# A gated feed-forward kernel: low parts of w_out computed by GpSimd, their smaller copy by ScalarE, and the matmul of w_out's bound placed two units later

## The chip, the cores and the metric

The kernel runs on one core of one Trainium2 chip. The metric is the device time of one execution in microseconds: the median of three runs of the kernel before is 1093.89 us (1093.72 to 1094.65). Where the text speaks of engines, TensorE does matmuls, VectorE and ScalarE do elementwise work, GpSimd is the slower elementwise engine (POOL in the profile), and SyncE issues the DMAs (SP). Each engine works through its own list of instructions in order; an instruction whose operand is not ready holds up all that stand behind it.

## What is computed

Two steps follow each other. The first mixes seven neighbouring rows of `x` with softmax weights, for each of 8 groups of 24 columns; the second is a feed-forward layer with a sigmoid gate.

```
w   = softmax(weight_gen, axis=-1)                 # [4, 4096, 8, 7]
out[b, s, h, :] = sum_k w[b, s, h, k] * x_pad[b, s + k, h, :]
y   = out.reshape(16384, 192)
h   = y @ w_in                                     # [16384, 2048]
g   = h / (1 + exp(-1.702 * h))
res = g @ w_out                                    # [16384, 192]
```

`w_in` (192 x 2048) and `w_out` (2048 x 192) arrive as 64-bit floats, the rest as 32-bit floats.

## The kernel before

The 16384 rows are cut into 32 blocks of 512. A block's mixed rows (tile `acc`) are made by GpSimd as seven products and six additions of 128 x 768 elements (`attend`, L150 and L165); its softmax (`softmax`, L129 to L144) wanders over VectorE (maximum, sum, reciprocal), GpSimd (subtract, multiply) and ScalarE (exponential). `scales` finds the block's largest magnitude on VectorE (L235 to L208), spreads it over all partitions by one small TensorE matmul into a tile `top` (L211), and makes scale factors of it. `split_x` and `turn` then write the block as pairs of half-precision numbers and transpose it by DMA.

The hidden layer is computed in units: unit (block, f) is one slice of 128 of the 2048 hidden columns, 16 units to a block. The text counts the units of block 0 from 0: unit 8 is slice 8. For each unit TensorE does four matmuls in `whole` (L390 to L393) and one in `halves` (L401 or L402) into a PSUM tile `h`; `gate` makes the tanh on ScalarE (`th`, L407) and the gated value on VectorE (`h`, L408); `split` writes it as two half-precision parts, the high one by ScalarE (`g`, L413) and the low one by VectorE (`g`, L414); and `second` multiplies these with three half-precision versions of `w_out`: `wos`, `wol` and `woh` (L424 to L426, 12 matmuls a unit). `woh` is `w_out` scaled and rounded, `wol` what the rounding left, and `wos` is `woh` times 2^-12.

The units go in groups of four: `whole` of the first and second, `halves` of all four, `gate` of the first, and so on. From the third group on, the matmuls of `second` for earlier units are put between them. The tiles `h` and `top` share a pool of five PSUM buffers.

All other work is put between the steps of the units by a table of numbers: `plan((2.3, 3.05, 3.1), bound_out())` means that the first step of `bound_out` is written into the program behind the point 2.3 units after the start, its second at 3.05, and so on. `until(n + 0.7)` in the loop over groups takes from the table what is due. So the table alone sets the order of the instructions on every engine.

`w_out` is prepared in six pieces of 512 columns. `narrow` makes 32-bit floats of the 64-bit ones, in the upper words of `raw_o`, so that a float lies in every second word; it also sums magnitudes. `bound_out` makes of these sums one scale factor `to_out` for all of `w_out`: VectorE reductions, the small matmul L211 into `top`, and a few VectorE operations on single columns (L216 to L352). Then `parts_out(c)` makes the three versions of piece c: `woh` by ScalarE (L357), `wol` by VectorE (L359), `wos` by VectorE (L377). All this stands between units 2 and 8 of block 0, where `second` first needs it.

Pairs of blocks share a tile `wb` of softmax weights; that of blocks 2 and 3 is subtracted by GpSimd (L131, once for each block) and exponentiated by ScalarE (L133, twice) while units 4 to 8 run, and `attend(2)` starts on GpSimd when the softmax of block 2 is done.

Of the kernel before, what the change touches and what calls it, by code (L numbers as in the profile page):

```python
# [14 lines left out]
AF = mybir.ActivationFunctionType  # L15
ALU = mybir.AluOpType
# [6 lines left out]
def conv_attention_then_ffn(  # L23
# [8 lines left out]
    nc = tc.nc  # L32
# [38 lines left out]
    woh, wol, wos = (const.tile([P, NF * D], F16, name=n) for n in ("woh", "wol", "wos"))  # L71
# [120 lines left out]
    scale = {}  # L192
    inv_w, unit = sc[:, 0:1], sc[:, 1:2]
    to_in, to_out = sc[:, 2:3], sc[:, 3:4]
# [24 lines left out]
    def power(e, to, inv, top):  # L219

        nc.vector.tensor_scalar(to.bitcast(I32), e, -1.0, top * ONE, ALU.mult, ALU.add)
        nc.vector.tensor_scalar(to.bitcast(I32), to.bitcast(I32), ONE, 253 * ONE, ALU.max, ALU.min)
        nc.vector.tensor_scalar(inv.bitcast(I32), to.bitcast(I32), -1.0, 254 * ONE, ALU.mult, ALU.add)
# [92 lines left out]
    narrowed = {}  # L316
# [21 lines left out]
    def bound(a0, a1, e):  # L338
        nc.vector.tensor_reduce(tops[1][:, 0:1], sums[:, a0:a1], axis=AX.X, op=ALU.max)
        yield from top_of(tops[1], e, True)  # L340
# [6 lines left out]
    def bound_out():  # L347

        e = sums[:, 14:15].bitcast(I32)
        yield from bound(6, 12, e)  # L350
        power(e, to_out, unit, 267)
        nc.vector.tensor_scalar(unit, unit, inv_w, 2.0**11, ALU.mult, ALU.mult)  # L352

    def parts_of(key, to, hi, lo):

        f = narrowed[key]
        nc.scalar.activation(hi, f, AF.Copy, scale=to)  # L357
        yield
        nc.vector.scalar_tensor_tensor(lo, f, to, hi, ALU.mult, ALU.subtract)  # L359

    def parts_in(c):
        s = slice(c * QC, (c + 1) * QC)
        yield from parts_of(("i", c), to_in, w0h[:, s], w0l[:, s])
# [8 lines left out]
                nc.sync.dma_start(to[h], tail[0][h * C1 : (h + 1) * C1, s].rearrange("d (q k) -> d q k", k=P))  # L372

    def parts_out(c):
        s = slice(c * QC, (c + 1) * QC)
        yield from parts_of(("o", c), to_out, woh[:, s], wol[:, s])
        nc.vector.tensor_scalar(wos[:, s], woh[:, s], 2.0**-12, None, ALU.mult)  # L377


    hp, th, gg, po, osb = {}, {}, {}, {}, {}  # L380
# [63 lines left out]
    def plan(slots, gen):  # L444
        for n in slots:
            todo.setdefault(math.floor(n), []).append((n, len(todo), gen))
# [20 lines left out]
    with tc.manual_schedule():  # L467
# [47 lines left out]
        plan((-2.5, -1.4), parts_tail(1))  # L515
        plan((-1.9, -0.7), parts_in(2))
        plan((-1.2, -0.06), parts_in(3))
        plan((2.3, 3.05, 3.1), bound_out())
        for c, slots in enumerate(((3.2, 3.6), (3.7, 4.1), (4.2, 4.7), (5.2, 5.7), (6.2, 6.7), (7.2, 7.7))):
            plan(slots, parts_out(c))  # L520
        plan((8.0,), scales_out(0))
        plan((8.2, 9.6, 9.7), scales(1))
# [121 lines left out]
```

## Time and profile before

| what | value |
|---|---|
| median of three runs | 1093.89 us |
| the profiled execution, its own time | 1095.54 us |
| its span | 1093.6 us |
| TensorE busy | 1053.7 us, 96% |
| VectorE, ScalarE, GpSimd busy | 834.6, 721.3 and 711.2 us |
| chain that ended last | 92% TensorE, 3% VectorE, 2% GpSimd, 2% ScalarE |

The profiled execution lies 1.94 us above its span and 1.65 us above the median. In the page's table of 40 slices TensorE is busy nine tenths or more from the third slice on, so the stretch before about 100 us is where other engines set the pace.

### The profile page before, as it was taken

What the parts mean: (1) busy time and instruction counts of PE and PEld (TensorE: products, weight loads), DVE (VectorE), ACT (ScalarE), POOL (GpSimd) and SP (SyncE); (2) the same over time, 40 slices, a digit from 0 to 9 for tenths busy, and PEclk for the clock granted to TensorE, in tenths of its full rate; (3) what the DMA queues carried; (4) which work ended last, traced back from release to release, by engine and by line L of the source; (5) the groups of instructions that cost most, each with busy time, mean ns of one, the idle gap of its engine ahead of it and who ended that gap; (6) DMA issues with size and microseconds to landing.
All of it is one profiled execution on the core that took longest, in us unless ns stands there. A gap on an engine that the chain in (4) does not pass through costs nothing.

```text
span 1093.6 us, 22203 instructions
## 1 busy us (share of the span) xinstructions
PE 1053.7 (96%) x8821; PEld 726.0 (66%) x8821; DVE 834.6 (76%) x1562; ACT 721.3 (66%) x1245; POOL 711.2 (65%) x483
## 2 busy tenths in 40 slices
PE   5399999999999999999999999999999999999998
PEld 4156666667676766666666666666666676767666
DVE  8787777787777777777778777777777777788765
ACT  5765766666666666666666666666666666666665
POOL 4439786666876666886666687666678766698000
PEclk9699999999999999999999999999999999999999
DMA  9300310312031021302112121121312102110110
GB/s 313 113 7 27 91 32 18 91 32 92 16 91 33 18 91 33 88 18 76 34 33 91 33 80 27 44 65 32 92 30 77 33 20 89 33 30 18 32 32 16
DMA packets 73232, 60.72 MB, mean 56 GB/s; under 512 B 60588, under 2 KB 65964, under 8 KB 71592
## 3 DMA queue, kind: packets, MB, share of 16 engines
q1 hardware_dynamic: 73128, 59.30, 18.9%
q8 instruction: 69, 1.13, 0.4%
q14 instruction: 35, 0.29, 0.1%
HBM read 31.96 MB, written 12.58 MB: 41 GB/s over the span
## 4 chain that ended last, share of the span: by engine, by line
PE 92%; DVE 3%; POOL 2%; ACT 2%; issue 1%; DMA 0%; POOLq 0%; ACTq 0%
PE o L424 16%; PE o L426 15%; PE o L425 15%; PE h L391 10%; PE h L392 10%; PE h L390 10%; PE h L393 10%; PE h L401 6%; POOL acc L165 1%; POOL prod L150 1%; PE tr L183 1%; DVE h L408 1%; ACT abs L336 1%; DVE g L414 0%; ACT bits L326 0%
## 5 line engine op out<-in xcount | busy, mean ns | idle before, releaser
L424 PE MATMUL o<-wos,g 128*128 128x192 f16 x2048 | 504.9, 247 | 0.0
L426 PE MATMUL o<-woh,g 128*128 128x192 f16 x2048 | 503.7, 246 | 0.0
L425 PE MATMUL o<-wol,g 128*128 128x192 f16 x2048 | 503.7, 246 | 0.0
L414 DVE SCALAR_TENSOR_TENSOR g<-g,h 128x512 f16<-128x512 f16 x512 | 340.1, 684 | 155.3 <-ACT g L413 147.0
L413 ACT ACTIVATE g<-h 128x512 f16<-128x512 f32 x512 | 305.7, 597 | 190.8 <-DVE h L408 190.7
L407 ACT ACTIVATE th<-h,s 128x512 f32<-128x512 f32 x512 | 337.0, 683 | 128.8 <-PE h L402 128.8
L408 DVE SCALAR_TENSOR_TENSOR h<-th,h 128x512 f32<-128x512 f32 x512 | 341.8, 690 | 82.9 <-ACT th L407 82.9
L165 POOL TENSOR_TENSOR acc<-acc,prod 128x768 f32<-128x768 f32 x186 | 338.1, 1817 | 14.6
L150 POOL TENSOR_TENSOR prod<-xb,wb 128x768 f32<-128x768 f32 x186 | 287.8, 1547 | 9.6
L424 PEld LDWEIGHTS <-g 128*128 128x128 f16 x2048 | 200.0, 98 | 97.6 <-issue 53.0
L425 PEld LDWEIGHTS <-g 128*128 128x128 f16 x2048 | 200.3, 98 | 40.9
L426 PEld LDWEIGHTS <-g 128*128 128x128 f16 x2048 | 200.3, 98 | 0.0
L390 PE MATMUL h<-xt,w0l 128*128 128x512 f16 x512 | 195.0, 381 | 0.5 <-DMA xt<-xs 0.5
L391 PE MATMUL h<-xt,w0h 128*128 128x512 f16 x512 | 195.1, 381 | 0.0
L392 PE MATMUL h<-xt,w0h 128*128 128x512 f16 x512 | 195.0, 381 | 0.0
L393 PE MATMUL h<-xt,wth 128*128 128x512 f16 x512 | 194.8, 380 | 0.0
L131 POOL TENSOR_TENSOR wb<-wb,wm 128x224 f32<-128x224 f32 x31 | 18.3, 592 | 237.4 <-DVE wm L129 237.4
L392 PEld LDWEIGHTS <-w0h 128*128 128x128 f16 x512 | 50.3, 98 | 61.0 <-issue 1.1
L393 PEld LDWEIGHTS <-wth 128*128 128x128 f16 x512 | 50.3, 98 | 61.0 <-issue 1.1
L402 PE MATMUL h<-xd,tl 64*128 64x512 f16 x256 | 77.7, 383 | 1.0 <-DVE g L414 1.0
L401 PE MATMUL h<-xt,tl 64*128 64x512 f16 x256 | 77.4, 383 | 0.0
L390 PEld LDWEIGHTS <-w0l 128*128 128x128 f16 x512 | 50.3, 98 | 3.0 <-issue 1.7
(91 smaller groups left out, 514.7 us busy)
## 6 DMA issues: line engine op xcount, KB each, us to landing
xb<-in_x_dram SPq DMA_DIRECT2D x12, 1344.0 KB, 6.3
out_dram<-osb SPq DMA_DIRECT2D x31, 384.0 KB, 2.6
wb<-in_weight_gen_dram SPq DMA_DIRECT2D x16, 224.0 KB, 3.2
ro<-in_moe_w_out_dram SPq DMA_DIRECT2D x4, 768.0 KB, 12.1
xb<-in_x_dram SPq DMA_DIRECT2D x3, 768.0 KB, 7.9
ri<-in_moe_w_in_dram SPq DMA_DIRECT2D x4, 512.0 KB, 8.2
xb<-in_x_dram SPq DMA_DIRECT2D x4, 504.0 KB, 5.9
xd<-xt SPq DMA_DIRECT2D x31, 64.0 KB, 2.1
```

The lines of the kernel that those rows point to most:

```text
L165: nc.gpsimd.tensor_tensor(acc, acc, t, ALU.add)
L390: nc.tensor.matmul(ps, lhsT=w0l[:, s], rhs=x0, start=start, stop=False)
L391: nc.tensor.matmul(ps, lhsT=w0h[:, s], rhs=x2, start=False, stop=False)
L392: nc.tensor.matmul(ps, lhsT=w0h[:, s], rhs=x0, start=False, stop=False)
L393: nc.tensor.matmul(ps, lhsT=th_[:, s], rhs=x1, start=False, stop=stop)
L407: nc.scalar.activation(t, hp[u], AF.Tanh, scale=scale[u[0]][:, 4:5])
L408: nc.vector.scalar_tensor_tensor(hp[u], t, 1.0, hp[u], ALU.add, ALU.mult)
L413: nc.scalar.activation(g[:, 0], hp[u], AF.Copy, scale=2.0**-12)
L414: nc.vector.scalar_tensor_tensor(g[:, 1], g[:, 0], -(2.0**12), hp.pop(u), ALU.mult, ALU.add)
L424: nc.tensor.matmul(o, lhsT=lo, rhs=wos[:, d], start=a and j % 2 == 0, stop=False, skip_group_check=True)
L425: nc.tensor.matmul(o, lhsT=hi, rhs=wol[:, d], start=False, stop=False, skip_group_check=True)
L426: nc.tensor.matmul(o, lhsT=hi, rhs=woh[:, d], start=False, stop=z, skip_group_check=True)
```

## The change

`parts_out` no longer goes through `parts_of`. ScalarE now first scales the piece in place in `raw_o`, then rounds it to `woh`, and later makes `wos` of it; GpSimd subtracts `woh` from the scaled piece, which gives `wol`. VectorE has no part in it any more. In the table of places, the second and third step of `bound_out`, which hold the matmul L211 and the single-column operations, go from 3.05 and 3.1 to 4.2 and 4.21, and the places of the six pieces go with them.

```diff
     def parts_out(c):
+
         s = slice(c * QC, (c + 1) * QC)
-        yield from parts_of(("o", c), to_out, woh[:, s], wol[:, s])
-        nc.vector.tensor_scalar(wos[:, s], woh[:, s], 2.0**-12, None, ALU.mult)
+        f = narrowed["o", c]
+        nc.scalar.activation(f, f, AF.Copy, scale=to_out)
+        nc.scalar.activation(woh[:, s], f, AF.Copy)
+        nc.gpsimd.tensor_tensor(wol[:, s], f, woh[:, s], ALU.subtract)
+        yield
+        nc.scalar.activation(wos[:, s], woh[:, s], AF.Copy, scale=2.0**-12)
...
-        plan((2.3, 3.05, 3.1), bound_out())
...
+        plan((2.3, 4.2, 4.21), bound_out())
...
```

Below the edit, lines of the changed kernel carry numbers that are higher by 5 (the tanh is L412 instead of L407, the high part L418 instead of L413). On TensorE the matmul L211 of `bound_out` stood directly ahead of unit 4's `whole`; it now stands behind `whole` of units 4 and 5 and `halves` of units 4 to 7. On VectorE the softmax maximum of block 3 and the gated value of unit 4 now stand ahead of L216 to L352. The next lists show ScalarE and GpSimd; the names end in the number of the buffer.

ScalarE, before, from the high part of unit 3 (`h_428`) to the tanh of unit 6; `h_493`, `h_498` and `h_503` are units 4, 5 and 6:

```order
L413 ACTIVATE g_475<-h_428 128x512
L357 ACTIVATE woh_97<-ro_112,sc_100 128x512 x2
L407 ACTIVATE th_509<-h_493,s_284 128x512
L357 ACTIVATE woh_97<-ro_112,sc_100 128x512
L407 ACTIVATE th_515<-h_498,s_284 128x512
L413 ACTIVATE g_518<-h_493 128x512
```

ScalarE in the changed kernel, from the same place; units 4 and 5 are `h_481` and `h_486` here:

```order
L418 ACTIVATE g_475<-h_428 128x512
L412 ACTIVATE th_497<-h_481,s_284 128x512
L378 ACTIVATE ro_112<-ro_112,sc_100 128x512
L379 ACTIVATE woh_97<-ro_112 128x512
L382 ACTIVATE wos_99<-woh_97 128x512
L412 ACTIVATE th_512<-h_486,s_284 128x512
L418 ACTIVATE g_515<-h_481 128x512
```

The tanh of unit 4 has moved ahead of the pieces of `w_out`, and each piece has three instructions in place of one, the second and third of which read what the one before them writes.

ScalarE, before, at the end of the stretch, from the tanh of unit 7 (`h_504`) to the tanh of unit 8 (`h_565`) and the exponentials of blocks 3 and 2 (`wb_137`, in this order):

```order
L407 ACTIVATE th_547<-h_504,s_284 128x512
L357 ACTIVATE woh_97<-ro_112,sc_100 128x512
L413 ACTIVATE g_553<-h_504 128x512
L357 ACTIVATE woh_97<-ro_112,sc_100 128x512
L133 ACTIVATE wb_137<-wb_137 128x224
L407 ACTIVATE th_607<-h_565,s_284 128x512
L133 ACTIVATE wb_137<-wb_137 128x224
```

ScalarE in the changed kernel there, from the second step of the fifth piece on; unit 7 is `h_492`, unit 8 `h_571`:

```order
L379 ACTIVATE woh_97<-ro_112 128x512
L418 ACTIVATE g_557<-h_492 128x512
L382 ACTIVATE wos_99<-woh_97 128x512
L378 ACTIVATE ro_112<-ro_112,sc_100 128x512
L379 ACTIVATE woh_97<-ro_112 128x512
L382 ACTIVATE wos_99<-woh_97 128x512
L133 ACTIVATE wb_137<-wb_137 128x224
L412 ACTIVATE th_613<-h_571,s_284 128x512
L133 ACTIVATE wb_137<-wb_137 128x224
```

The exponentials and the tanh of unit 8 still stand behind all pieces, of which each is now three instructions long.

GpSimd, before, from the last two additions for block 1 (`acc_256`) to the first product for block 2 (`acc_629`); `wm_523` belongs to block 2, `wm_490` to block 3:

```order
L165 TENSOR_TENSOR acc_256<-acc_256,prod_411 128x768
L150 TENSOR_TENSOR prod_414<-xb_119,wb_117 128x768
L165 TENSOR_TENSOR acc_256<-acc_256,prod_414 128x768
L131 TENSOR_TENSOR wb_137<-wb_137,wm_523 128x224
L131 TENSOR_TENSOR wb_137<-wb_137,wm_490 128x224
L144 TENSOR_TENSOR wb_137<-wb_137,wr_524 128x224
L150 TENSOR_TENSOR acc_629<-xb_139,wb_137 128x768
```

GpSimd in the changed kernel; `wm_521` belongs to block 2, `wm_478` to block 3:

```order
L165 TENSOR_TENSOR acc_256<-acc_256,prod_414 128x768
L380 TENSOR_TENSOR wol_98<-ro_112,woh_97 128x512 x2
L131 TENSOR_TENSOR wb_137<-wb_137,wm_521 128x224
L380 TENSOR_TENSOR wol_98<-ro_112,woh_97 128x512 x4
L131 TENSOR_TENSOR wb_137<-wb_137,wm_478 128x224
L144 TENSOR_TENSOR wb_137<-wb_137,wr_522 128x224
L150 TENSOR_TENSOR acc_635<-xb_139,wb_137 128x768
```

The subtraction for block 3, for which the first of the two exponentials waits, has come to stand behind the low parts of all six pieces.

## Rows read from the trace of the kernel before

**Rows 1.** Busy time of each engine in two stretches: length, busy time and instructions of PE, PEld, DVE, ACT and POOL, then the granted TensorE clock as a share of full speed, the share of the DMA engines and GB/s.

```profile
54.00:58.10 4.10, 4.10 (x12) 1.04 (x11) 2.35 (x10) 1.56 (x3) 0.00 (x0) 0.52 0.00 0
...
99.00:1090.00 991.00, 990.85 (x8402) 685.09 (x8402) 755.27 (x1394) 657.76 (x1127) 659.74 (x435) 1.00 0.17 48
```

**Rows 2.** Waits of TensorE between 40 and 110 us: who waited for whom, us in total, times, longest.

```profile
PE top L211 <- DVE tf L206: 6.6, 1, 6.6
PE top L211 <- DVE tf L208: 3.6, 2, 1.9
```

**Rows 3.** TensorE in order of time: start in us, length, what it did, and in brackets how long the engine had been idle and who released it. The matmul at 46.71 is the last of units 0 to 3, the one at 68.22 the last of unit 10, that at 72.90 the last of unit 11.

```profile
46.71 0.38 PE L393 MATMUL h<-xt,wth 128*128 128x512 f16 x1
...
53.67 0.19 PE L211 MATMUL top<-tf,ones 128*128 128x4 bf16 x1 [6.58 <-DVE tf L206]
...
68.22 0.38 PE L393 MATMUL h<-xt,wth 128*128 128x512 f16 x1
...
70.24 0.18 PE L211 MATMUL top<-tf,ones 128*128 128x1 bf16 x1 [1.64 <-DVE tf L208]
...
72.90 0.38 PE L393 MATMUL h<-xt,wth 128*128 128x512 f16 x1
...
96.84 0.38 PE L393 MATMUL h<-xt,wth 128*128 128x512 f16 x1
...
99.16 0.18 PE L211 MATMUL top<-tf,ones 128*128 128x1 bf16 x1 [1.94 <-DVE tf L208]
```

**Rows 4.** The chain that ended last, in order of time: start, length, what. Between the first two of these rows the chain has GpSimd rows only.

```profile
73.04 0.58 POOL wb L144
...
95.84 1.81 POOL acc L165
97.68 0.96 DVE top L235
```

**Rows 5.** VectorE in order of time. The row at 53.52 is the low part of unit 3, that at 68.05 the gated value of unit 8; L222 finishes the factor `to_out`.

```profile
53.52 0.68 DVE L414 SCALAR_TENSOR_TENSOR g<-g,h 128x512 f16<-128x512 f16 x1
54.12 0.15 DVE L216 TENSOR_REDUCE tm<-top 128x1 f32<-128x4 f32 x1
...
54.68 0.15 DVE L222 TENSOR_SCALAR sc<-sc 128x1 int32<-128x1 int32 x1
...
56.52 0.38 DVE L129 TENSOR_REDUCE wm<-wb 128x32 f32<-128x224 f32 x1
...
68.05 0.69 DVE L408 SCALAR_TENSOR_TENSOR h<-th,h 128x512 f32<-128x512 f32 x1
...
77.79 0.37 DVE L129 TENSOR_REDUCE wm<-wb 128x32 f32<-128x224 f32 x1
```

**Rows 6.** ScalarE in order of time. The tanh at 67.27 is that of unit 8, the one at 74.56 that of unit 11.

```profile
52.86 0.60 ACT L413 ACTIVATE g<-h 128x512 f16<-128x512 f32 x1 [0.78 <-DVE h L408]
54.87 1.39 ACT L357 ACTIVATE woh<-ro,sc 128x512 f16<-128x512 f32 x2 [1.42 <-DVE sc L222]
...
58.51 0.75 ACT L357 ACTIVATE woh<-ro,sc 128x512 f16<-128x512 f32 x1
59.16 0.67 ACT L407 ACTIVATE th<-h,s 128x512 f32<-128x512 f32 x1
59.73 0.59 ACT L413 ACTIVATE g<-h 128x512 f16<-128x512 f32 x1
60.21 0.76 ACT L357 ACTIVATE woh<-ro,sc 128x512 f16<-128x512 f32 x1
...
66.99 0.39 ACT L133 ACTIVATE wb<-wb 128x224 f32<-128x224 f32 x1
67.27 0.68 ACT L407 ACTIVATE th<-h,s 128x512 f32<-128x512 f32 x1
...
74.56 0.68 ACT L407 ACTIVATE th<-h,s 128x512 f32<-128x512 f32 x1
```

**Rows 7.** ScalarE's groups of instructions by line and shape: count, busy us, mean ns of one, idle time before.

```profile
L413 ACT ACTIVATE g<-h 128x512 f16<-128x512 f32 x512 | 305.7, 597 | 190.8 <-DVE h L408 190.7
...
L275 ACT ACTIVATE xs<-acc,s 128x768 f16<-128x768 f32 x31 | 29.0, 934 | 0.0
...
L357 ACT ACTIVATE woh<-ro,sc 128x512 f16<-128x512 f32 x6 | 4.4, 750 | 1.4 <-DVE sc L222 1.4
L336 ACT ACTIVATE abs<-ro 128x512 bf16<-128x512 f32 x6 | 3.9, 654 | 0.8 <-DVE ro L332 0.8
L328 ACT ACTIVATE m<-ro 128x512 f32<-128x512 f32 x6 | 3.7, 620 | 0.0
```

**Rows 8.** GpSimd's groups in the same view.

```profile
L165 POOL TENSOR_TENSOR acc<-acc,prod 128x768 f32<-128x768 f32 x186 | 338.1, 1817 | 14.6
L150 POOL TENSOR_TENSOR prod<-xb,wb 128x768 f32<-128x768 f32 x186 | 287.8, 1547 | 9.6
...
L131 POOL TENSOR_TENSOR wb<-wb,wm 128x224 f32<-128x224 f32 x31 | 18.3, 592 | 237.4 <-DVE wm L129 237.4
```

**Rows 9.** The lines L377 and L359, each in the view of one line: count, shortest, median and longest duration in ns, first and last start in us.

```profile
L377 DVE TENSOR_SCALAR wos<-woh x6: 282/283/286, 56.3 to 67.8; 128x512 f16<-128x512 f16 x6
...
L359 DVE SCALAR_TENSOR_TENSOR wol<-ro,sc,woh x6: 742/744/750, 55.7 to 67.2; 128x512 f16<-128x512 f32 x6
```

**Rows 10.** GpSimd in order of time: the subtraction for block 4, between the products for block 2.

```profile
78.58 1.02 POOL L131 TENSOR_TENSOR wb<-wb,wm 128x224 f32<-128x224 f32 x1
```

More of the change, by code (lines that the diff above doesn't have):

```diff
@@ L517, in conv_attention_then_ffn @@
         plan((-1.2, -0.06), parts_in(3))
-        plan((2.3, 3.05, 3.1), bound_out())
-        for c, slots in enumerate(((3.2, 3.6), (3.7, 4.1), (4.2, 4.7), (5.2, 5.7), (6.2, 6.7), (7.2, 7.7))):
+        plan((2.3, 4.2, 4.21), bound_out())
+        for c, slots in enumerate(((4.22, 4.5), (4.75, 5.2), (5.5, 6.05), (6.2, 6.7), (6.9, 7.2), (7.25, 7.7))):
             plan(slots, parts_out(c))
```

## The prediction

> **What bounds the kernel now.** I began with the busy time by stretch. From 99 us to 1090 us TensorE is busy for 990.85 of 991 us [rows 1]: once past 99 us it never waits, and no change ahead of that point can alter what it still has to do. So the end is the moment at which TensorE passes 99 us, plus a constant, and the question is only what sets that moment. The waits of TensorE come next [rows 2]: one of 6.6 us for the bound of w_out, and two, 3.6 us together, for the scale of a block. In order of time [rows 3] the first lies from 47 to 53.67 us, the second, of 1.64 us, ends with the matmul at 70.24, and the third, of 1.94 us, with that at 99.16. The third is the one that counts: whatever TensorE gains earlier makes this wait longer and nothing else, unless the matmul at 99.16 can itself start sooner.
>
> What does it wait for? The chain [rows 4] answers: VectorE's reduction at 97.68 over the finished block 2, and ahead of it GpSimd without a gap since 73.04, where the softmax of block 2 is multiplied out and `attend(2)` begins. Seven products and six additions later the block is there. So the start of that GpSimd chain, 73.04, sets the end of the kernel. It is set in turn by VectorE and ScalarE: the gated value of unit 8 at 68.05 [rows 5], then, in VectorE's fixed order, the scale of block 1, the softmax sum, the gated value of unit 9 and the reciprocal. That takes 73.04 - 68.05 = 4.99 us and is not edited. At 68.05 VectorE was just then free, while the tanh it needs had started at 67.27 and taken 0.68 [rows 6], so it was ready 0.1 us before. Both engines are nearly level there.
>
> **The change part by part.** Taken away from VectorE are six `wol` of 0.744 and six `wos` of 0.283 us [rows 9], 6.16 us in all ahead of 68.05. Added to GpSimd are six subtractions. ScalarE had six `woh` of 0.75 [rows 7] and now has eighteen operations. Nothing else is added; no DMA is issued at another place in its queue, and the bank that unit 8's matmul gets is still the one that `top` leaves.
>
> The matmul two units later: TensorE no longer stops at 47 us, it goes on with units 4 to 7 as their PSUM buffers come free. But the matmul L211 now writes where unit 3 was, so it waits for the low part of unit 3, 53.52 + 0.68 = 54.20. Behind it on VectorE, L216 stands after one softmax maximum (0.38 [rows 5]) and the gated value of unit 4. With successive VectorE rows starting 0.08 before the other has ended (53.52 + 0.68 against 54.12), that is 0.30 + 0.61, about 0.9 us. `to_out` was there at 54.68 + 0.15 and ScalarE began 0.04 later, at 54.87 [rows 6]; now it begins at 54.87 + 0.89 = 55.76. So the factor comes no earlier but a little later: it hangs on VectorE's work on unit 3, not on TensorE.
>
> From 55.76 on ScalarE has no pause, and its work is the term that decides. One piece is: the scaling, like L357 in operands, 0.75, and 0.04 of handing over, because the next operation reads what it wrote; the rounding, without a scale column, like L336 and L328, 0.65 [rows 7], and 0.04; then `wos`, as long as L413, 0.62 at most, whose end may overlap the next by 0.09 (58.51 + 0.75 against 59.16), so 0.53. That makes 0.79 + 0.69 + 0.53 = 2.01, six times 12.06, less 0.13 in the one place where unit 7's high part stands between two of them: 11.93. Between the pieces stand three tanh and four high parts, from start to start 0.57 and 0.48 (59.16, 59.73, 60.21), together 3.63. The last `wos` is issued by 55.76 + 11.93 + 3.63 = 71.32, and the last `woh` is finished at 70.75.
>
> A new wait follows. The first exponential waits for GpSimd's subtraction for block 3, which now stands behind the sixth `wol`, which waits for the last `woh`. A subtraction of 512 elements is not in the trace; by the addition of 768 in 1.817 it is 1.21, by the product 1.03, and a whole addition of 1.82 is my upper end [rows 8]. I take 1.2, the nearest in form. So 70.79 + 1.2 + 0.59 for L131, with two handovers 72.66; the exponential at 72.66, the tanh of unit 8 0.28 later (66.99 to 67.27), finished at 73.62, the gated value at 73.66. Before it was 68.05: **5.6 us later**, and the GpSimd chain starts 5.6 us later with it. VectorE's 6.16 us are saved where VectorE then only waits.
>
> What hides nothing of this: TensorE reaches the end of unit 10 (68.22) at about the same time as before, since what it needs there, the low part of unit 6 and three pieces, is done by 66 us in the walk above. It then stands still until the matmul now at 70.24 runs at about 75.9, some 7 us. After the idle 6.58 us of before, the granted clock was 0.52 for the next 4.1 us [rows 1], that is the 1.2 GHz level. I expect the same, and it costs up to 2.05 us of TensorE's time. Unit 11 would then be ready at 72.90 + 0.38 + 5.6 + 2.05 = 80.9, 0.8 after its tanh could start (74.56 + 5.6). The maximum for block 4 stands behind that on VectorE and ends at 77.79 + 0.37 + 5.6 + 0.8 = 84.56, where GpSimd's L131 would have been ready at 78.58 + 5.6 = 84.18 [rows 5, 10]. So GpSimd loses **0.4 us** more. TensorE itself arrives at 96.84 + 0.22 + 5.6 + 2.05 = 104.7, before the 99.1 + 6.0 = 105.1 at which the third wait ends; the 1.94 us of slack cover the clock.
>
> The sum is +5.6 + 0.4 = +6.0 us. For the profiled execution that is 1095.54 + 6.0 = 1101.5; the median lies 1.65 below that execution, so 1093.89 + 6.0 = **1099.9 us**.
>
> The bounds: the scaling in place is in no row, nor is a read of half-precision numbers by ScalarE. If each of the eighteen took only the 0.48 at which high parts follow each other, and GpSimd 1.03, the last `woh` would be done at 67.5 and the gated value at 70.2: +2.2. If the scaling took the 0.934 of L275 and the other two 0.75 each with their handover, a piece is 2.5, ScalarE is 3 us later, and with 1.82 on GpSimd the sum is +9.6.
>
> Two rules of the Trainium skill bear on ScalarE's term. The trace shows a pair of `woh` in 1.39 us, 0.11 less than twice 0.75 [rows 6]. ScalarE: Activation LUTs, section "What ACT_TABLE_LOAD costs", says that activations back to back overlap by about 93 ns. If this held for operations that read each other's result as well, twelve handovers of 0.04 and twelve overlaps would fall away, and the sum would be some 4.4 us instead of 6.0. No row of this case has such a pair on ScalarE. The same page's "Rules for kernel authors" says to use VectorE, not ScalarE, for plain multiplies, which can be up to three times slower in half precision: by it a `wos` of 0.283 would be 0.85 on ScalarE, and the sum 1.4 us more.
>
> **The rivals.** (a) *ScalarE's operations overlap.* If operations that depend on each other overlap as independent ones do (0.10 by the rows above) and need no handover, the sum falls by 12 x 0.14 = 1.7 to about +4.3, 1098.2 us. For it speaks the 1.39 for a pair [rows 6], against it that those two do not read each other. (b) *The clock costs more.* If TensorE stays at the lower level twice as long as the 4.1 us of [rows 1], because it is fed in spurts, it loses 4.1, arrives 1.6 after the scale of block 2 is ready, and unit 11 delays GpSimd by two more: about +8, 1102 us. Against it speaks that TensorE has a full queue after the wait. (c) *Faster: VectorE was the limit and ScalarE is not.* Then VectorE's saved 6.16 us count, and the tanh of unit 4 can follow the high part of unit 3 at 52.86 + 0.48 instead of standing behind two pieces. With pieces at the 0.65 each of the old `woh`, ScalarE would be through at 55.76 + 3.9 + 3.6 = 63.3 and unit 8's gated value near 64.3: -3.7, 1090.2 us. It decides from the point where the eighteen take under 11.93 - 5.6 = 6.3 us, 0.35 each; nothing of 512 columns in the trace follows another within 0.48. (d) *No change.* The eighteen at 0.46 to 0.48 each and a quick GpSimd bring unit 8 to within 2.2 us of 68.05; the same rows speak against it.
>
> **How the numbers follow.** The forecast, ScalarE's pieces with the wait behind them, has 0.66, and its own range is 1098.7 to 1101.5. (a) has 0.14, (b) 0.12, (c) 0.04 and (d) 0.04. The three runs of before spread by 0.09%; I count a difference as real from 0.2%, 2.2 us, on. Forecast, (a) and (b) are slower, 0.92; the same 0.04; faster 0.04. From the bounds of +2.2 and +9.6 and the spans of (a) and (b) I take 1096.6 to 1103.2 as the range.
>
> **What would show it.** In the new profile, ScalarE should run without idle time from about 55.8 to 71 us, with a handover visible between the three operations of a piece; the first exponential should wait for GpSimd near 72.7; the tanh of unit 8 should start near 73; the 6.6 us wait of TensorE for the bound should be gone and one of about 7 us for the scale of block 1 be there instead, with a lower granted clock after it; `attend(2)` should start near 78.6 and the third wait end near 105. I am wrong if the gated value of unit 8 comes before 70.2, or if it comes late and TensorE nevertheless passes the third matmul L211 near 99 us.

## The result, and the profile after

The changed kernel takes 1101.38 us (median of 6 runs, 1100.29 to 1102.29); the kernel before takes 1094.27 in its 6 runs (1093.39 to 1095.25). The ratio is 1.0064, with a 95% interval of 1.0051 to 1.0077, that is 5.6 to 8.4 us more. The profiled execution has a span of 1099.5 us against 1093.6, and 1101.45 us of its own time.

Busy time by stretch, with the columns of [rows 1]:

```profile
70.00:76.00 6.00, 0.82 (x7) 0.78 (x8) 2.36 (x6) 2.62 (x7) 1.68 (x2) 0.57 0.00 0
76.00:80.00 4.00, 4.00 (x24) 3.28 (x22) 3.58 (x12) 2.51 (x5) 1.95 (x2) 0.50 0.01 4
...
105.00:1096.00 991.00, 990.86 (x8402) 685.08 (x8402) 755.17 (x1393) 657.12 (x1128) 659.00 (x435) 1.00 0.17 48
```

The last line has the same length, and almost to the instruction the same contents, as that from 99 us on in [rows 1]: everything behind it is a copy, and the whole difference was made ahead of 105 us. The first line is new: TensorE is busy 0.82 of 6 us.

The waits of TensorE from 40 to 110 us, to be held against [rows 2]:

```profile
PE top L211 <- DVE tf L208: 7.8, 2, 7.1
PE h L407 <- DVE g L419: 2.8, 2, 1.6
PE top L211 <- DVE g L419: 1.6, 1, 1.6
PE o L429 <- ACT wos L382: 1.3, 1, 1.3
```

The 6.6 us for the bound are gone (1.6 are left, for the low part of unit 3), and the waits for the scale of a block have grown from 3.6 to 7.8. TensorE in order of time, the first row being the first `halves` of unit 0, the others answering to [rows 3]:

```profile
44.10 0.39 PE L406 MATMUL h<-xt,tl 64*128 64x512 f16 x1
...
53.69 0.19 PE L211 MATMUL top<-tf,ones 128*128 128x4 bf16 x1 [1.60 <-DVE g L419]
...
75.18 0.19 PE L211 MATMUL top<-tf,ones 128*128 128x1 bf16 x1 [7.14 <-DVE tf L208]
...
80.30 0.63 PE L398 MATMUL h<-xt,wth 128*128 128x512 f16 x1
...
105.02 0.18 PE L211 MATMUL top<-tf,ones 128*128 128x1 bf16 x1 [0.67 <-DVE tf L208]
```

The same `halves` in the kernel before:

```profile
44.65 0.39 PE L401 MATMUL h<-xt,tl 64*128 64x512 f16 x1
```

So this execution was 0.55 us ahead before anything that is edited ran. From a common start the third matmul L211 comes 105.02 - 99.16 + 0.55 = 6.4 us later, which lies between the 5.9 of the two spans and the 7.1 of the medians; no profile shows where the other 0.7 of the 7.1 lies. Positions below are compared with that 0.55 taken off the forecast.

ScalarE, the first and the last piece of `w_out`, the exponential of block 3 and the tanh of unit 8; compare [rows 6]:

```profile
55.20 0.76 ACT L378 ACTIVATE ro<-ro,sc 128x512 f32<-128x512 f32 x1 [1.74 <-DVE sc L222]
55.98 0.66 ACT L379 ACTIVATE woh<-ro 128x512 f16<-128x512 f32 x1
56.67 0.63 ACT L382 ACTIVATE wos<-woh 128x512 f16<-128x512 f16 x1
57.21 0.67 ACT L412 ACTIVATE th<-h,s 128x512 f32<-128x512 f32 x1
...
69.54 0.65 ACT L379 ACTIVATE woh<-ro 128x512 f16<-128x512 f32 x1
70.22 0.63 ACT L382 ACTIVATE wos<-woh 128x512 f16<-128x512 f16 x1
71.98 0.39 ACT L133 ACTIVATE wb<-wb 128x224 f32<-128x224 f32 x1 [1.13 <-POOL wb L131]
72.28 0.67 ACT L412 ACTIVATE th<-h,s 128x512 f32<-128x512 f32 x1
```

Between 55.20 and 70.85 ScalarE has no row with a bracket: it never waits, and sets the pace there. Then it waits 1.13 us for GpSimd. GpSimd from the sixth low part on ([rows 4, 10] before):

```profile
70.27 1.15 POOL L380 TENSOR_TENSOR wol<-ro,woh 128x512 f16<-128x512 f32 x1 [1.16 <-ACT woh L379]
71.38 0.57 POOL L131 TENSOR_TENSOR wb<-wb,wm 128x224 f32<-128x224 f32 x1
77.97 0.58 POOL L144 TENSOR_TENSOR wb<-wb,wr 128x224 f32<-128x224 f32 x1 [6.03 <-DVE wr L141]
...
84.47 1.01 POOL L131 TENSOR_TENSOR wb<-wb,wm 128x224 f32<-128x224 f32 x1 [0.90 <-DVE wm L129]
```

The bracket of 0.90 at 84.47 was not there before. VectorE's gated value of unit 8 stands at 72.98 instead of 68.05 [rows 5]; it had waited 3.91 us for the tanh.

```profile
72.98 0.70 DVE L413 SCALAR_TENSOR_TENSOR h<-th,h 128x512 f32<-128x512 f32 x1 [3.91 <-ACT th L412]
```

### The profile page after: what moved, and what is told of

It is laid out like the page before. It is cut to its first block, busy times and chain, and to the rows that moved or that the text cites. A ratio compares the mean times of both kernels' runs of the same rounds, so it can differ in the third digit from the quotient of the medians.

```text
span 1099.5 us, 22208 instructions
## 1 busy us (share of the span) xinstructions
PE 1056.2 (96%) x8821; PEld 727.8 (66%) x8821; DVE 829.7 (75%) x1550; ACT 728.0 (66%) x1257; POOL 717.5 (65%) x489
## 3 DMA queue, kind: packets, MB, share of 16 engines
q8 instruction: 69, 1.13, 0.4%
## 4 chain that ended last, share of the span: by engine, by line
PE 92%; ACT 3%; DVE 2%; POOL 2%; issue 1%; DMA 0%; ACTq 0%
PE o L429 16%; PE o L431 15%; PE o L430 15%; PE h L396 10%; PE h L395 10%; PE h L398 10%; PE h L397 10%; PE h L406 6%; POOL acc L165 1%; POOL prod L150 1%; PE tr L183 1%; ACT abs L336 1%; ACT bits L326 0%; ACT ro L378 0%; ACT woh L379 0%
## 5 line engine op out<-in xcount | busy, mean ns | idle before, releaser
L418 ACT ACTIVATE g<-h 128x512 f16<-128x512 f32 x512 | 305.6, 597 | 186.8 <-DVE h L413 186.7
L412 ACT ACTIVATE th<-h,s 128x512 f32<-128x512 f32 x512 | 336.5, 682 | 130.4 <-PE h L407 129.0
L413 DVE SCALAR_TENSOR_TENSOR h<-th,h 128x512 f32<-128x512 f32 x512 | 341.9, 690 | 89.6 <-ACT th L412 89.6
L131 POOL TENSOR_TENSOR wb<-wb,wm 128x224 f32<-128x224 f32 x31 | 18.3, 589 | 226.1 <-DVE wm L129 226.1
L407 PE MATMUL h<-xd,tl 64*128 64x512 f16 x256 | 77.5, 381 | 2.8 <-DVE g L419 2.8
```

Of the source, the lines that this page charges most:

```text
L412: nc.scalar.activation(t, hp[u], AF.Tanh, scale=scale[u[0]][:, 4:5])
L413: nc.vector.scalar_tensor_tensor(hp[u], t, 1.0, hp[u], ALU.add, ALU.mult)
L418: nc.scalar.activation(g[:, 0], hp[u], AF.Copy, scale=2.0**-12)
```

## The experiments

The theory: ScalarE's eighteen operations, and GpSimd's subtraction for block 3 behind the sixth low part, make unit 8 late; with it the start of GpSimd's work on block 2 and the third wait of TensorE. The rivals: the new table of places does it, or the lower clock after the long wait. All ten runs are told here. "Third matmul" is the L211 of block 2.

**The two halves of the change apart.** The first run has only the new table, the second only the new engines:

```diff
         s = slice(c * QC, (c + 1) * QC)
-        f = narrowed["o", c]
-        nc.scalar.activation(f, f, AF.Copy, scale=to_out)
...
+        yield from parts_of(("o", c), to_out, woh[:, s], wol[:, s])
+        nc.vector.tensor_scalar(wos[:, s], woh[:, s], 2.0**-12, None, ALU.mult)
```

> The changed table of places, with the engines of before: ScalarE makes woh in one operation, VectorE wol and wos. Theory (ScalarE's eighteen operations in a row, and the wait for GpSimd behind them, hold up the tanh of unit 8 and with it the GpSimd chain for block 2): without the eighteen, VectorE's row is the longest again. From 56.0 us it has six wol and wos at 0.87 from start to start, seven operations of units 4 to 7 at 0.6 and one maximum of 0.3, 9.7 us, with about 1 us of waits: the gated value of unit 8 near 66.5 instead of 68.05, and the time 1 to 2 us below that of before. Rival (the moved matmul is what costs, through TensorE's order and its clock): about 5 to 7 us above before, as in the changed kernel.

```diff
-        plan((2.3, 4.2, 4.21), bound_out())
+        plan((2.3, 3.05, 3.1), bound_out())
...
```

> The changed engines, with the table of before. Theory: ScalarE begins the pieces at 54.9, 0.3 to 0.9 earlier than in the changed kernel, but now has unit 4's tanh behind that, so its last woh is done at about 70.4, the tanh of unit 8 starts near 72.5 and the time is 5 to 6.5 us above before, like the changed kernel within 1 us. Rival (the moved matmul is what costs): within 1 us of before.

The engines alone take 1101.04 us, ratio 1.0053 (1.0039 to 1.0067), 6.5 above the kernel before, as expected: the loss is theirs, although TensorE's 6.6 us wait for the bound is back in that run. The gated value of unit 8 and the third matmul:

```profile
72.71 0.70 DVE L412 SCALAR_TENSOR_TENSOR h<-th,h 128x512 f32<-128x512 f32 x1 [3.42 <-ACT th L411]
```

```profile
104.75 0.18 PE L211 MATMUL top<-tf,ones 128*128 128x1 bf16 x1 [0.56 <-DVE tf L208]
```

The table alone takes 1094.98, ratio 1.0000 (0.9991 to 1.0009), where a gain of 1 to 2 was expected. Unit 8 did come early (66.60, expected 66.5), and the third matmul ran at 97.70, 1.46 us earlier, or 1.27 from a common start (44.46 against 44.65 at the first `halves`). But the gain was lost behind it. The table's run by stretch, and two of its TensorE rows:

```profile
97.70:100.00 2.30, 2.30 (x16) 1.55 (x17) 2.24 (x4) 1.73 (x3) 2.22 (x2) 0.70 0.00 0
100.00:102.00 2.00, 2.00 (x12) 1.55 (x11) 1.86 (x9) 1.22 (x4) 1.92 (x2) 0.50 0.00 0
102.00:1090.00 988.00, 988.00 (x8378) 682.89 (x8375) 750.31 (x1382) 654.21 (x1123) 654.81 (x432) 1.00 0.17 48
```

```profile
97.70 0.18 PE L211 MATMUL top<-tf,ones 128*128 128x1 bf16 x1 [1.94 <-DVE tf L208]
...
98.81 0.63 PE L391 MATMUL h<-xt,w0l 128*128 128x512 f16 x1
```

After a wait of 1.94 us the granted clock went to 0.50, the 1.2 GHz level, for some 3.4 us (0.30 x 2.3 x 2 + 2.0); in the kernel before a wait of the same 1.94 us [rows 3] was followed by a clock of 1.00. From the third matmul to the end of the span it takes 1093.8 - 97.70 = 996.1 us here; in the kernel before, the changed one, and the other nine runs it takes 994.4 or 994.5. So 1.6 us were lost there, about half of the 3.4 us at the lower level.

**Does that clock account for the table's lost gain?** The same kernel with TensorE kept busy in the third wait (the fillers' result is overwritten by the matmul behind them):

```diff
         ps = ps_h.tile([P, N], F32, tag="h", name="top")
+        for _ in range(fill):
+            nc.tensor.matmul(ps, lhsT=w0h[:, 0:P], rhs=w0h[:, 0:N], start=True, stop=True)
...
-        yield from top_of(t, e, False)
+        yield from top_of(t, e, False, 8 if blk == 2 else 0)
```

> The run with the changed table and the engines of before, with 8 filler matmuls of 512 columns (about 1.7 us) ahead of the small matmul of block 2, in its wait of 1.94 us; they change no output. Theory (the 1.46 us that the table gains were taken back by the lower clock that TensorE was granted after that wait): third matmul near 97.7 as in that run, whole units behind it at 0.38 a matmul, clock 1.00 from 98 to 102, time 1.3 to 1.6 us below the kernel before, about 1092.9 where it has 1094.4. Rival (something else behind 99 us took them back): the clock stays up but the time equals the kernel before within 0.3.

It took 1093.60 us against 1094.71 of the kernel before, ratio 0.9989 (0.9980 to 0.9998). The granted clock behind the third matmul was 1.00, and from there the span takes 994.5 us again. So the clock had taken back the table's gain. It is 1.1 us and not the expected 1.3 to 1.6, because the fillers ended late: the third matmul is at 98.25, in an execution that was 0.20 behind at the first `halves` (44.66 against 44.46), so 0.35 us later than in the table's run.

**One operation back.** The changed kernel with `wos` on VectorE:

```diff
-        nc.scalar.activation(wos[:, s], woh[:, s], AF.Copy, scale=2.0**-12)
+        nc.vector.tensor_scalar(wos[:, s], woh[:, s], 2.0**-12, None, ALU.mult)
```

> The changed kernel with wos made by VectorE again (12 operations on ScalarE for the pieces instead of 18). Theory: 6 x 0.53 = 3.2 us fewer on ScalarE, all of it ahead of the tanh of unit 8, so 3.2 us below the changed kernel, or up to 0.9 us more where TensorE's shorter wait lets GpSimd's 0.9 us wait go: 2 to 3.5 us above before. Rival (the moved matmul is what costs): no more than 0.5 us below the changed kernel.

1098.79 us, ratio 1.0034 (1.0022 to 1.0046): 2.6 below the changed kernel by the medians, 2.8 by the spans. That leaves it 4.2 above the kernel before, where 2 to 3.5 was expected. Unit 8 came 2.7 us earlier, at 70.26, or 3.0 from a common start (44.38 against 44.10), of the 3.2 expected. The wait of the exponential grew from 1.13 to 1.89 us, mostly because ScalarE no longer fills 0.63 of it with the sixth `wos`, and GpSimd's wait for block 4, which might have gone, stayed:

```profile
69.26 0.39 ACT L133 ACTIVATE wb<-wb 128x224 f32<-128x224 f32 x1 [1.89 <-POOL wb L131]
```

```profile
81.72 1.01 POOL L131 TENSOR_TENSOR wb<-wb,wm 128x224 f32<-128x224 f32 x1 [0.88 <-DVE wm L129]
```

TensorE had waited 6.10 us for the scale of block 1, and behind that wait stayed at the lower level for some 5.5 us:

```profile
72.46:78.00 5.54, 5.54 (x29) 4.23 (x30) 4.37 (x13) 3.06 (x6) 2.67 (x3) 0.50 0.01 3
```

**The new wait taken away.** The changed kernel with block 3's subtraction ahead of the sixth low part:

```diff
-                plan((3.7, 7.75, 7.8, 11.7, 13.7, 17.6), softmax(blk, G_))
+                plan((3.7, 7.22, 7.8, 11.7, 13.7, 17.6), softmax(blk, G_))
```

> The changed kernel with GpSimd's subtraction for block 3 one place earlier, ahead of the sixth wol. Theory: the first exponential no longer waits (1.13 us of ScalarE's idle time in the changed kernel), the tanh of unit 8 starts 1.1 to 1.2 us earlier, and the time is 1.1 to 1.3 us below the changed kernel. Rival (ScalarE's and GpSimd's lateness is covered by TensorE's own late arrival, because the lower clock has used up its slack): no difference.

1098.74 us, ratio 1.0035 (1.0021 to 1.0049): 2.6 below by the medians and 2.0 by the spans, more than expected. ScalarE and GpSimd of this run:

```profile
70.88 0.37 ACT L133 ACTIVATE wb<-wb 128x224 f32<-128x224 f32 x1
...
78.98 0.69 ACT L412 ACTIVATE th<-h,s 128x512 f32<-128x512 f32 x1 [0.49 <-PE h L398]
```

```profile
76.86 0.58 POOL L144 TENSOR_TENSOR wb<-wb,wr 128x224 f32<-128x224 f32 x1 [5.31 <-DVE wr L141]
82.41 1.02 POOL L131 TENSOR_TENSOR wb<-wb,wm 128x224 f32<-128x224 f32 x1
```

The exponential no longer waits, the GpSimd chain starts 1.1 us earlier, and the wait of 0.90 for block 4 is gone as well, since unit 11's tanh waited 0.49 us instead of 1.43. My expectation counted the first and left out the second. The second is the clock's: behind a wait of 5.92 us TensorE was at the lower level for some 3.7 us, and not for the 5.7 of the changed kernel.

```profile
74.06:77.80 3.74, 3.74 (x25) 3.53 (x26) 2.87 (x7) 2.47 (x5) 0.87 (x2) 0.50 0.02 4
```

The length of the wait does not decide this alone, because with `wos` on VectorE a wait of 6.10 us was followed by 5.5 us at that level. So 1.1 us of this run's gain is shown to be the edit's, and what made the stretch shorter stays open.

**The clock after the long wait.** The changed kernel with 30 fillers, in the same place but for block 1:

```diff
-        yield from top_of(t, e, False)
+        yield from top_of(t, e, False, 30 if blk == 1 else 0)
```

> The changed kernel, with 30 filler matmuls of 512 columns (about 6.4 us at full clock) written into the bank of the small matmul L211 of block 1, ahead of it, where TensorE stands idle for 7.14 us; they change no output. Theory (the lower clock after the long wait makes unit 11 late, and GpSimd's subtraction for block 4 waits 0.90 us for it): the granted clock stays at 1.00 behind 75 us, the matmuls of unit 11 take 0.38 instead of 0.63, the tanh of unit 11 waits less than 0.5, GpSimd's wait of 0.90 falls below 0.1, the third wait's matmul runs near 104.1 instead of 105.02 after a wait of 1.5 to 2.5 us, and the time is 0.9 us below the changed kernel, about 1100.4. Rival (the clock after this wait costs the end nothing): third matmul near 105.0, time within 0.3 of the changed kernel. Second rival (the longer third wait lowers the clock behind it, as in the run with the table alone): third matmul near 104.1, but 0 to 0.8 us above the changed kernel's time.

```profile
70.00:76.00 6.00, 5.85 (x28) 2.67 (x29) 1.99 (x6) 3.07 (x6) 1.81 (x3) 1.00 0.01 3
76.00:80.00 4.00, 4.00 (x40) 3.17 (x39) 3.13 (x8) 2.47 (x5) 0.89 (x2) 1.00 0.00 0
```

By stretch the clock stays at 1.00, and TensorE does 40 matmuls from 76 to 80 us where the changed kernel did 24. GpSimd's subtraction for block 4 has no wait. The third matmul is at 105.13 after 1.76 us of waiting, in an execution that was 1.03 us behind the changed kernel's at the first `halves` (45.13 against 44.10): 104.10 from a common start, the expected 104.1. The time, 1100.73, ratio 1.0053 (1.0038 to 1.0067), is 0.65 below the changed kernel's, with overlapping intervals. So the rows of this one execution show the 0.9 us, and the times alone would not.

**The chain started much earlier.** The table's run with block 2's softmax some four units earlier:

```diff
-                plan((4.8, 4.81, 8.1, 8.5, 8.8, 9.1), softmax(blk, G_))
-                plan([9.2 + 1.5 * k for k in range(K)], attend(blk))
+                plan((3.7, 3.71, 4.215, 4.3, 4.45, 4.46), softmax(blk, G_))
+                plan([5.0 + 0.5 * k for k in range(K)], attend(blk))
...
-                plan((3.7, 7.75, 7.8, 11.7, 13.7, 17.6), softmax(blk, G_))
+                plan((4.8, 4.81, 7.8, 11.7, 13.7, 17.6), softmax(blk, G_))
```

> The run with the changed table and the engines of before, and besides: the softmax of block 2 ahead of the one of block 3 and about four units earlier, so that GpSimd starts on the products for block 2 near 60 to 63 us instead of 71.6, while units 4 to 8 run. Theory (the start of that GpSimd chain alone sets the third wait, and TensorE has about 2 us of slack there): the third wait is gone or under 0.3, TensorE passes the third matmul near 96 to 97.2, the time is 1.5 to 3.3 us below the kernel before, about 1091 to 1093. Rival (the end hangs on TensorE's own arrears from the waits before 75 us): the third wait is gone, yet the time is within 0.5 of the kernel before. What would hurt: the earlier softmax makes VectorE late with units 4 to 8, by 1 us at most.

A miss, and not a small one: 1101.89 us, ratio 1.0067 (1.0054 to 1.0080). The third wait is gone as expected, but TensorE comes there at 105.2, because its second wait grew to 9.62 us. VectorE shows why:

```profile
68.18 1.76 DVE L359 SCALAR_TENSOR_TENSOR wol<-ro,sc,woh 128x512 f16<-128x512 f32 x1
69.86 1.63 DVE L378 TENSOR_SCALAR wos<-woh 128x512 f16<-128x512 f16 x1
71.41 2.35 DVE L359 SCALAR_TENSOR_TENSOR wol<-ro,sc,woh 128x512 f16<-128x512 f32 x1
73.69 1.63 DVE L378 TENSOR_SCALAR wos<-woh 128x512 f16<-128x512 f16 x1
75.23 0.68 DVE L409 SCALAR_TENSOR_TENSOR h<-th,h 128x512 f32<-128x512 f32 x1
```

While GpSimd makes its products and additions, a `wos` takes 1.63 us instead of 0.283 and a `wol` up to 2.35 instead of 0.744 [rows 9]; the gated value keeps its 0.68. Together the twelve operations on the pieces take 9.2 us longer. Unit 8 came at 75.23. The expectation priced this at 1 us at most; from 66.60 in the table's run it was 8.6. GpSimd beside them:

```profile
67.58 1.80 POOL L165 TENSOR_TENSOR acc<-acc,prod 128x768 f32<-128x768 f32 x1
69.46 1.87 POOL L150 TENSOR_TENSOR prod<-xb,wb 128x768 f32<-128x768 f32 x1
71.41 1.80 POOL L165 TENSOR_TENSOR acc<-acc,prod 128x768 f32<-128x768 f32 x1
73.29 1.87 POOL L150 TENSOR_TENSOR prod<-xb,wb 128x768 f32<-128x768 f32 x1
```

The ends fit together: each of the two `wos` ends 0.16 us after the product that ran beside it (71.49 against 71.33, 75.32 against 75.16), and each `wol` 0.55 or 0.56 after the addition (69.94 against 69.38, 73.76 against 73.21). So the rows read as a wait for the end of GpSimd's operation, and not as work at a lower rate.

**The chain started a little earlier, with no piece left on VectorE.** In the table's run VectorE did the gated value of unit 9 and a low part between block 2's sum and its reciprocal, and had waited 0.87 us ahead of the first of them. The reciprocal now stands right behind the sum:

```diff
-                plan((4.8, 4.81, 8.1, 8.5, 8.8, 9.1), softmax(blk, G_))
-                plan([9.2 + 1.5 * k for k in range(K)], attend(blk))
+                plan((4.8, 4.81, 8.1, 8.5, 8.51, 8.52), softmax(blk, G_))
+                plan([8.55 + 1.05 * k for k in range(K)], attend(blk))
```

> The run with the changed table and the engines of before, and besides: VectorE's reciprocal for block 2 directly behind its sum, ahead of the gated value of unit 9, GpSimd's multiplication and the products behind it, and the places of the products 1.05 units apart, so that the subtraction for block 4 falls later among them. No piece of w_out is left on VectorE when GpSimd starts. Theory (the start of the GpSimd chain sets the end of the wait at the third matmul, and VectorE is idle 0.87 us behind the sum): the multiplication starts 1.8 to 1.9 us earlier than with the table alone, near 69.8, the third wait falls from 1.94 to under 0.3, the granted clock does not fall behind it, TensorE passes the third matmul near 96, and from there to the end of the span 994.5 us pass: 2.0 to 2.8 us below the kernel before, about 1092. Rival (GpSimd's products slow VectorE's work on units 9 to 11, or the subtraction for block 4 waits, so that the wait stays): third wait over 1 us, time within 1 us of the kernel before.

As expected: 1092.55 us against 1095.00, ratio 0.9979 (0.9970 to 0.9988), 2.4 us below the kernel before. GpSimd's multiplication is at 69.47, TensorE has no third wait, and the third matmul runs at 96.44:

```profile
69.47 0.58 POOL L144 TENSOR_TENSOR wb<-wb,wr 128x224 f32<-128x224 f32 x1 [8.73 <-DVE wr L141]
```

```profile
96.44 0.17 PE L211 MATMUL top<-tf,ones 128*128 128x1 bf16 x1
```

A second step on top of it, the maximum of block 1 ahead of the sixth piece:

```diff
-        plan((8.2, 9.6, 9.7), scales(1))
+        plan((7.6, 9.6, 9.7), scales(1))
```

> As the run with the early reciprocal, and the maximum of block 1 on VectorE ahead of the sixth piece of w_out instead of behind the gated value of unit 8. Theory (TensorE's second wait, 2.7 us for that maximum, is slack that counts as soon as the third wait is gone): the matmul of block 1 runs about 1.6 us earlier, the gated value of unit 8 1.3 us later, the reciprocal at the same time as there, third wait up to 1.9 us again, so that the end is set by GpSimd once more: the same time as that run within 0.5 us. Rival (the delay of unit 8 passes on to the GpSimd chain): 1.0 to 1.5 us slower than that run.

The time is the same, 1092.87, ratio 0.9980 (0.9971 to 0.9989), but not for the reason expected: the third wait did not come back. TensorE's second wait fell from 2.70 to 1.11, and a new one stood in the way, for the transposed rows of block 1:

```profile
PE h L391 <- DMA xt<-xs: 3.0, 1, 3.0
```

Behind that wait the granted clock was 0.77 from 84 to 88 us. This execution was also 1.52 us ahead of the one before it at the first `halves` (42.99 against 44.51), and its third matmul is at 96.80. From a common start that is 1.9 us later, where the medians differ by 0.3; so the profile shows a place where the gain went, and does not account for the equal times.

**The changed kernel mended.** `wos` on VectorE, block 3's subtraction earlier, and the early reciprocal with its products, by the edits above:

```diff
-        nc.scalar.activation(wos[:, s], woh[:, s], AF.Copy, scale=2.0**-12)
+        nc.vector.tensor_scalar(wos[:, s], woh[:, s], 2.0**-12, None, ALU.mult)
...
-                plan((4.8, 4.81, 8.1, 8.5, 8.8, 9.1), softmax(blk, G_))
+                plan((4.8, 4.81, 8.1, 8.5, 8.51, 8.52), softmax(blk, G_))
...
-                plan((3.7, 7.75, 7.8, 11.7, 13.7, 17.6), softmax(blk, G_))
+                plan((3.7, 7.22, 7.8, 11.7, 13.7, 17.6), softmax(blk, G_))
...
```

> The changed kernel with three repairs: wos by VectorE, the subtraction for block 3 ahead of the sixth low part, and the reciprocal and products of block 2 earlier as in the run with the early reciprocal; low parts by GpSimd, scaling and rounding by ScalarE. Theory (all the loss comes from the lateness of unit 8, and the repairs add up: 2.6 and 2.6 us by their medians, 1.9 for the reciprocal): gated value of unit 8 near 69.3, start of the GpSimd chain near 72.1, third matmul near 98, time 5.5 to 7.0 us below the changed kernel, 1094.4 to 1095.9. Rival (the two repairs of unit 8 share their gain, because VectorE's wos makes GpSimd's low parts longer and the wait for GpSimd returns): unit 8 above 70, time 1096.5 or more.

1095.24 us, ratio 1.0001 (0.9992 to 1.0010), 6.1 us below the changed kernel: the repairs add up to about what was expected. Unit 8 is at 68.69 and the GpSimd chain starts at 71.85, both a little sooner than expected. The third matmul, however, is at 100.6 and not near 98: TensorE no longer waits there but comes late itself, after a second wait of 4.26 us and a granted clock of 0.54 from 70 to 76 us:

```profile
70.89 0.19 PE L211 MATMUL top<-tf,ones 128*128 128x1 bf16 x1 [4.26 <-DVE tf L208]
...
100.56 0.17 PE L211 MATMUL top<-tf,ones 128*128 128x1 bf16 x1
```

That profiled execution, of 1096.79 us, was the slowest of its 11 (1093.26 to 1096.79). One of the three repairs, the early reciprocal, has nothing to do with the change: with it and the old engines the kernel takes 1092.55 us. Against that run the mended change is still 2.7 us slower, and its unit 8 is still 2.4 us later (68.69 against 66.32). So the change is not free even so.

## Why the prediction was right

The path was right: the change is slower, through unit 8 and GpSimd's work on block 2, and the run of the engines alone shows that it is the engines' doing. The steps, in the order of the chain, with the 0.55 us of the earlier start taken off the forecast:

| step | forecast | measured |
|---|---|---|
| ScalarE begins with the pieces | 55.21 | 55.20 |
| last `woh` finished | 70.20 | 70.19 |
| exponential of block 3 | 72.11 | 71.98 |
| gated value of unit 8 | 73.11 | 72.98 |
| GpSimd chain for block 2 begins | 78.1 | 77.97 |
| third matmul | 104.6 | 105.02 |

That the profiled execution took 1101.45 us, with 1101.5 forecast, is luck: the sum was 0.4 us too small, and the execution started 0.55 early. The median came out 1.5 above the forecast of 1099.9: 0.4 of it is that sum, 0.4 that the kernel before has 1094.27 in six runs, and 0.7 is in no profile.

**What sets the end.** Twelve profiles bear on the step "the third matmul plus a constant": eleven have 994.4 or 994.5 us behind it. The twelfth, the table alone, has 1.6 more, by the clock. So the step held for the change, whose third wait was only 0.67 us, but it was stated too strongly, since a wait of 1.94 us has been followed by either level of the clock.

**The factor no earlier.** Right to 0.01 us. The engines with the old table take 1101.04 us and with the new one 1101.38, so the new table gives the change nothing.

**ScalarE's pieces.** The forecast of 0.79 + 0.69 + 0.53 for a piece from start to start was 0.78 + 0.69 + 0.54 for the first one (55.20, 55.98, 56.67, 57.21). An operation that reads the result of the one ahead starts 0.02 or 0.03 after its end; one that does not starts 0.09 ahead of it (56.67 + 0.63 against 57.21). This decides the first place where the Trainium skill was weighed: the overlap of ScalarE: Activation LUTs, "What ACT_TABLE_LOAD costs", is seen between independent operations only, and the sum of 4.4 us by it falls, with rival (a). The second place, "Rules for kernel authors" of the same page, points the right way: `wos` took 0.63 on ScalarE against 0.283 on VectorE, and putting it back gained 2.6 us. The factor that this page of the Trainium skill gives is "up to about 3×", per element and for bf16. The prediction took it for the whole operation in f16, an estimate of 0.85 us; here the factor was 2.2.

**The new wait.** 1.15 us for a low part, where 1.2 was taken, and 0.57 for L131. Taking it away moved the start of the GpSimd chain 1.1 us forward, as the 1.13 of the exponential says.

**The clock, and GpSimd's second loss.** This is the mis-sized term. The long wait came as forecast (7.14 us, "some 7"). Behind it TensorE stayed at the lower level from 75.18 to about 80.9, the end of the matmul at 80.30, which is 5.7 us and not 4.1. So unit 11's tanh waited 1.43 us instead of 0.8, and GpSimd lost 0.90 instead of 0.4: the sum of +6.0 should have been +6.4. The run with 30 fillers shows that this 0.9 is the clock's doing, and in the run with the earlier subtraction, where the stretch was 3.7 us, it was gone. Rival (b), that the clock would cost two more, was right that the stretch would be longer, but 5.7 us is not twice 4.1, and TensorE still arrived 0.67 us before the scale of block 2 was ready. The prediction's sum for that arrival takes 0.22 us for the matmul at 96.84, whose row [rows 3] has 0.38; with that it is 104.9 instead of 104.7. TensorE came at 105.02 - 0.67 + 0.55 = 104.9, and that is luck too: the lower clock cost some 0.8 us more than the 2.05, and 0.5 of it was made up because a wait of the kernel before is not there in the changed one:

```profile
PE h L390 <- DMA xt<-xs: 0.5, 1, 0.5
```

**Faster or no change.** Rivals (c) and (d) needed eighteen operations of 0.35, or at most 0.48 each; the three of a piece took 0.76, 0.66 and 0.63, or 0.78, 0.69 and 0.54 from start to start.

## What to carry to other kernels

Work moved off an engine that waits anyway gains nothing where the receiving engine stands in front of a chain that sets the end; walk that engine's queue, instruction by instruction, to the first one that somebody else waits for. Then look at what that one instruction stands behind: here two places in a table (a reciprocal 0.3 units earlier with the steps behind it, a subtraction half a unit earlier) came with 2 us and more each, part of it through the clock. And where a wait of TensorE gets shorter or longer, count the clock behind it as a term of its own, about half the time that it stays low (1.6 us of 3.4 in the table's run).

## What was not expected

- The pieces of `w_out` on VectorE took up to six times as long while GpSimd made its products and additions (`wos` 1.63 instead of 0.283, `wol` 2.35 instead of 0.744), while VectorE's gated values (0.68) and the maximum over a block (0.93) kept theirs; by the ends of the rows they stood until GpSimd's operation was over. It also works the other way: GpSimd's products took 1.87 instead of 1.55 beside the pieces, and its low part 1.26 instead of 1.15 when `wos` was on VectorE. So GpSimd's idle stretch ahead of block 2 cannot be filled for nothing as long as the pieces are on VectorE. What in the operands makes the difference was not tried. The Trainium skill, GPSIMD Engine Reference, "1. Specifications", says that GpSimd shares its interfaces to SBUF with VectorE, and contends with VectorE's instructions that run in a mode with two ports or have two SBUF inputs; the trace agrees, since the `wol` has two inputs in SBUF, the gated value one in PSUM, and the maximum a single input. The `wos` has a single input as well, and no row shows which mode it ran in.
- A wait of 1.94 us was followed by full clock in one kernel and by some 3.4 us at the lower level in another. Waits of 5.92 and 6.10 us were followed by 3.7 and 5.5. What tells these cases apart was not looked for, and stays open.
